# A weight copy moved from GpSimd to a DMA, and a denser output projection for half of a layer

## The chip, the cores and the metric

The kernel runs on one core of one Trainium2 chip. Five engines work side by side, each through its own instructions in order: TensorE (PE in the profile, its weight loads PEld), VectorE (DVE), ScalarE (ACT), GpSimd (POOL) and SyncE (SP), which here issues nearly all DMAs. They wait for one another through semaphores. The metric is the device time in microseconds; lower is better. The time before is 382.32 us, the median of 3 runs (382.29 to 382.58).

## The reference

Two layers of sliding dilated attention alternate with two gated feed-forward layers, all on x of 2048 tokens by 448 channels (bf16), with the same weights both times:

```python
def A(x):   # 16 heads of 28 channels, window of 8 keys, every second token
    q, k, v = split_heads(x @ wqkv)
    idx = pos[:, None] - 2 * arange(8)[None, :]
    attn = softmax(where(idx >= 0, q . k[idx] * 28 ** -0.5, -1e9))
    return merge_heads(attn . v[idx]) @ wo

def B(x):
    return ((x @ w_gate) * (x @ w_up)) @ w_down     # 448 -> 1792 -> 448

x = x + A(layernorm(x)); x = x + B(layernorm(x))
x = x + A(layernorm(x)); x = x + B(layernorm(x))
```

## The kernel before, in words

The four layers are numbered 0 to 3 (0 and 2 attention, 1 and 3 feed-forward). Tokens lie in 16 blocks of 128 (`NBLK`); x stays in `x_sb` through all layers. A layer is worked in chunks of 256 or 512 tokens, and `SEQ` (line 62) interleaves the chunks of different layers, so that TensorE has feed-forward matmuls while an attention chunk waits for softmax.

Everything is recorded as operations with dependencies (`Sched.add`). Which engine does an operation, and in which order each engine goes, is written out by hand-off tables: `ORDER` (line 104) lists operation numbers for each engine, `BANKS` (line 168) the PSUM banks. `Sched.emit` puts out each engine's list with the semaphore waits that the dependencies ask for. An engine never takes a later operation before an earlier one; that holds for SyncE's DMA list too.

TensorE mostly works on the array cut in two halves of 64 rows (line 363): two matmuls run at the same time, and I call such a pair a step. Score matmuls (line 855) and attention-value matmuls (line 889) are short and use small tiles of the array, eight at a time; a group of 64 of them is called a burst. In an entry of `ORDER` such as `551*3.5/349:1+350:1`, steps of other work (here the down projection) are cut into strips of 32 columns (line 366) and put between the parts of a burst; a burst without such strips is called bare here.

The attention of a pair of blocks ends like this. Values times weights (`AV`) go from PSUM to `O_sb` (line 900), a shuffle spreads the denominators (line 918), ScalarE makes their reciprocals by logarithm and exponential (lines 919 and 920), and VectorE multiplies them in and writes `oT` (line 931, called `N`). Then `y_blocks` (line 946 on) does the output projection of two blocks, and `x_block` (line 971) adds it to x on VectorE (line 972).

A head has 28 channels but takes 32 partitions in `oT`, so 16 heads fill 4 chunks of 128 partitions with 4 rows of each 32 unused. In layer 0 the projection runs over these 4 chunks, 512 rows, with zeros in the unused rows of the weights `wo_g`: 8 steps for a pair of blocks. In layer 2 the last four heads are moved into the unused rows: one DMA (line 949, `M0`) stores them from `oT` to DRAM, four (line 953, `M1`) load them back into rows 28 to 31 of each 32, and the weights are put in the same order, in `wo_g` for one block of the pair and in a second copy `wo_h` for the other. That makes 448 rows, 7 steps.

`wo_h` begins as a copy of `wo_g` made by GpSimd (line 556, `c_wh`). Ten small DMAs (`wp`, lines 557 to 569) then fill the unused rows of both. They depend on the copy and on all layer-0 projections (`Y0`), since those need the zeros.

Of the kernel before, what the change touches and what calls it, by code (L numbers as in the profile page):

```python
# [14 lines left out]
NBLK = S // 128  # L15
NCH = S // 512
QB = 120
NQB = 17
# [41 lines left out]
FILL = 9  # L60
ATT_P = 3.0
# [35 lines left out]
def grp_nc(g):  # L97
# [22 lines left out]
    ),  # L120
    "act": (
# [12 lines left out]
    ),  # L134
    "dve": (
# [18 lines left out]
    ),  # L154
    "pool": (
        "18 19 38 20 21 22 23 24 25 26 27 28 29 30 31 32 33 34 35 36 37 92"
# [235 lines left out]
def build(nc, A_x, A_wqkv, A_wo, B_w_gate, B_w_up, B_w_down, out):  # L392
# [25 lines left out]
    wo_g = sb([128, 4, D], bf, "wo_g")  # L418
# [31 lines left out]
    def one(fn, key=None):  # L450
        return [(fn, key)]
# [702 lines left out]
```

## Time and profile before

| | |
|---|---|
| median of 3 runs | 382.32 us |
| the profiled execution's own time | 381.71 us |
| its span, first to last instruction | 380.0 us |
| granted TensorE clock | 1.00 |
| busy: TensorE / VectorE / ScalarE / GpSimd | 374.5 / 283.6 / 206.2 / 6.5 us |

The profile is one execution. A row of groups gives the line of the kernel, engine, operation, what is written and read, and the count, then busy time and the mean duration of one in ns, then the idle time before and what ended it. A timeline row gives start and duration in us. In the chain of waits, each piece is what the next one waited for, or the instruction before it on its engine; "issue" is time in which nothing that the profile shows was waited for.

### The profile page before, as it was taken

To read this page: it belongs to the slowest core of one execution; us is meant where nothing else is said; L and a number is where in the kernel's file an instruction comes from. 1 tells how busy PE (TensorE), PEld (TensorE's weight loads), DVE (VectorE), ACT (ScalarE), POOL (GpSimd) and SP (SyncE) were. 2 spreads that over 40 slices of the span, in tenths; PEclk is the share of its full clock that TensorE was granted. 3 is DMA by queue.
4 is the path that set the end of the run, shared out by engine and by line. 5 is a ranking of instruction groups with operands and counts; after the bars stand their busy time and mean duration, and the time that the engine had idled before them with its cause. 6 is when DMAs were issued, how large, how long until landed. Compare 5 with 4: busy or idle time off the path is not lost.

```text
span 380.0 us, 14476 instructions
## 1 busy us (share of the span) xinstructions
PE 374.5 (99%) x6396; PEld 213.9 (56%) x6396; DVE 283.6 (75%) x640; ACT 206.2 (54%) x393; POOL 6.5 (2%) x26
## 2 busy tenths in 40 slices
PE   8999999999999999999999999999999999999997
PEld 4654487544555444554867765555555444445764
DVE  7999999989795677858677886746998588275423
ACT  5896997655536462535555524547856544134310
POOL 5001000000000000000000000000000000000000
PEclk9999999999999999999999999999999999999999
DMA  7667542500411023151104215310233103302003
GB/s 263 164 152 174 97 120 55 106 10 14 96 29 30 4 54 65 18 83 32 25 15 59 43 28 97 57 27 3 58 68 60 45 3 76 46 2 50 3 2 133
DMA packets 57850, 23.40 MB, mean 62 GB/s; under 512 B 47356, under 2 KB 57788, under 8 KB 57788
## 3 DMA queue, kind: packets, MB, share of 16 engines
q1 hardware_dynamic: 57644, 22.42, 27.5%
q8 instruction: 50, 0.82, 0.9%
q14 instruction: 12, 0.10, 0.1%
q10 hardware_dynamic: 144, 0.06, 0.1%
HBM read 8.91 MB, written 3.24 MB: 32 GB/s over the span
## 4 chain that ended last, share of the span: by engine, by line
PE 92%; ACT 3%; DVE 3%; DMA 1%; issue 0%; SPq 0%; DVEq 0%
PE ps L363 83%; PE ps L366 4%; PE ps L855 2%; PE ps L889 2%; PE ps L1023 1%; ACT E_sb L864 1%; DVE oT L931 1%; DMA x_sb<-in_A_x_dram 1%; ACT qk L730 0%; ACT R_sb L919 0%; ACT R_sb L920 0%; PE ps L635 0%; DVE R_sb L918 0%; DVE E_sb L871 0%; DVE xn_sb L621 0%
## 5 line engine op out<-in xcount | busy, mean ns | idle before, releaser
L363 PE MATMUL ps<-xnTb,WGU 64*128 64x512 bf16 (+1 forms) x1902 | 173.9, 333 | 0.1
L363 PEld LDWEIGHTS ps<-xnTb,WGU 64*128 64x128 bf16 x1902 | 93.4, 94 | 69.1 <-issue 1.0
L1008 ACT ACTIVATE g_sb<-ps 128x512 bf16<-128x512 f32 (+1 forms) x140 | 70.5, 510 | 92.0 <-PE ps L363 85.6
L1011 DVE TENSOR_TENSOR hT<-g_sb,ps 128x512 bf16<-128x512 bf16 (+1 forms) x140 | 78.4, 576 | 49.0 <-ACT g_sb L1008 48.1
L363 PE MATMUL ps<-WD,hT 64*128 64x448 bf16 x786 | 80.4, 350 | 0.0
L363 PEld LDWEIGHTS ps<-WD,hT 64*128 64x128 bf16 x786 | 40.1, 94 | 31.6 <-issue 0.3
L363 PE MATMUL ps<-xnTa,WQK 64*128 64x512 bf16 (+1 forms) x494 | 53.2, 353 | 0.6 <-DVE xnTa L645 0.5
L972 DVE TENSOR_TENSOR x_sb<-x_sb,ps 128x448 bf16<-128x448 bf16 x62 | 36.4, 614 | 19.6 <-PE ps L363 19.5
L864 ACT ACTIVATE E_sb<-ps,shift_sb 128x1024 bf16<-128x1024 f32 (+1 forms) x36 | 37.3, 1069 | 17.1 <-PE ps L855 16.9
L600 DVE BATCH_NORM_STATS2 st<-x_sb 128x6 f32<-128x448 bf16 x64 | 38.2, 616 | 1.2 <-DMA x_sb<-in_A_x_dram 0.7
L621 DVE TENSOR_SCALAR xn_sb<-x_sb,mv,rstd 128x512 bf16<-128x512 bf16 (+1 forms) x64 | 35.0, 569 | 1.5 <-ACT rstd L605 1.2
L363 PEld LDWEIGHTS ps<-xnTa,WQK 64*128 64x128 bf16 x494 | 23.9, 94 | 20.8 <-DVE xnTa L645 0.7
L730 ACT ACTIVATE qk<-ps 128x1024 bf16<-128x1024 f32 (+1 forms) x29 | 27.2, 948 | 13.8 <-PE ps L363 13.5
L363 PE MATMUL ps<-wo_g,oT 64*128 64x448 bf16 x184 | 26.8, 350 | 0.9 <-DVE oT L931 0.9
L871 DVE TENSOR_TENSOR E_sb<-E_sb,MK 128x1024 bf16<-128x1024 bf16 (+1 forms) x36 | 23.1, 657 | 5.2 <-ACT E_sb L864 5.1
L931 DVE TENSOR_TENSOR oT<-O_sb,R_sb 128x480 bf16<-128x480 f32 (+3 forms) x36 | 23.0, 656 | 3.2 <-ACT R_sb L920 3.1
L900 ACT ACTIVATE O_sb<-ps 128x512 f32<-128x512 f32 (+2 forms) x24 | 12.8, 564 | 21.5 <-PE ps L889 21.5
L363 PE MATMUL ps<-WV,xnTa 64*128 64x336 bf16 (+3 forms) x244 | 23.4, 305 | 0.1
L918 DVE STREAM_SHUFFLE R_sb<-O_sb 128x480 f32<-128x480 f32 (+1 forms) x34 | 22.9, 693 | 0.0
L919 ACT ACTIVATE R_sb<-R_sb 128x480 f32<-128x480 f32 (+1 forms) x34 | 19.9, 600 | 4.4 <-DVE R_sb L918 4.2
L920 ACT ACTIVATE R_sb<-R_sb 128x480 f32<-128x480 f32 (+1 forms) x34 | 19.9, 599 | 0.2
L855 PEld LDWEIGHTS ps<-Qz,qk 64*32 64x32 bf16 (+1 forms) x912 | 12.5, 94 | 7.7 <-issue 3.0
(68 smaller groups left out, 232.6 us busy)
## 6 DMA issues: line engine op xcount, KB each, us to landing
out_dram<-x_sb SPq DMA_DIRECT2D x15, 112.0 KB, 1.8
x_sb<-in_A_x_dram SPq DMA_DIRECT2D x3, 448.0 KB, 5.6
hT<-in_A_wqkv_dram SPq DMA_DIRECT2D x4, 224.0 KB, 4.3
WGU<-in_B_w_gate_dram SPq DMA_DIRECT2D x4, 224.0 KB, 3.7
WGU<-in_B_w_up_dram SPq DMA_DIRECT2D x4, 224.0 KB, 3.8
WD<-in_B_w_down_dram SPq DMA_DIRECT2D x2, 448.0 KB, 3.7
WGU<-in_B_w_gate_dram SPq DMA_DIRECT2D x2, 336.0 KB, 4.9
WGU<-in_B_w_up_dram SPq DMA_DIRECT2D x2, 336.0 KB, 4.4
```

The costliest lines, as they stand in the source:

```text
L363: return lambda E: E.matmul(out(), lhs(), rhs(), start=start, stop=stop)
L600: sc.add("dve", one(lambda E, B=B: E.bn_stats(st6[:, B, :], x_sb[:, B, :]), ("bn", li, B)), 525.0, deps=[("x", li - 1, B)] + ([("xn", li - ...
L621: sc.add("dve", one(lambda E, B=B, dst=dst, src=src: E.tensor_scalar(dst, src, mv[:, B, 0:1], rstd[:, B:B + 1], ALU.subtract, ALU.mult), ( ...
L730: return E.activation(dst, src, ACT.Copy) if hasattr(E, "activation") else E.tensor_copy(dst, src)
L855: ins.append((lambda E, hc=hc, c=c, s_=s_, p=p, b=b, h=h, ks=ks, qs=qs, lo=lo, hi=hi: E.matmul(ps[64 * c + KN * s_:64 * c + KN * s_ + KN, ...
L864: return E.activation(E_sb[:, slot, 2 * hp:2 * hp + 2, 0:w], ps[:, b0:b0 + 2, 0:w], ACT.Exp, bias=shift_sb[:, 0:1], scale=SCALE)
L871: return E.tensor_tensor(e, e, MK[:, kind, 0:nc].unsqueeze(1).unsqueeze(1).to_broadcast([128, 2, w // nc, nc]), ALU.min)
L918: sc.add("dve", one(lambda E: E.stream_shuffle(R, Of, [DH] * 32), ("Rs", li, qb)), dve_est(w) + 20.0, deps=[("Oa", li, g)] + prev, prio=prio)
L931: return E.tensor_tensor(oT[:, :, a % HALF:a % HALF + z - a], O[:, :, a - tok:z - tok], R.rearrange("p (h n) -> p h n", h=4)[:, :, a - tok ...
L972: sc.add("dve", one(lambda E: E.tensor_tensor(x_sb[:, B, :], x_sb[:, B, :], ps[:, bk[w], 0:D], ALU.add), ("x", li, B)), dve_est(D), deps=[ ...
L1008: sc.add("act", one(lambda E, gs=gs, bk=bk: E.activation(g_sb[:, gs, 0:nt], ps[:, bk[0], 0:nt], ACT.Copy), ("G", li, j, fc)), act_est(nt), ...
L1011: sc.add("dve", one(lambda E, gs=gs, bk=bk, fc=fc: E.tensor_tensor(hT[:, fc, hs, 0:nt], g_sb[:, gs, 0:nt], ps[:, bk[1], 0:nt], ALU.mult), ...
```

## The change

The copy of `wo_g` into `wo_h` becomes a DMA on SyncE's queue. `Y0`, the projections for which the ten small weight loads wait, shrinks to those of blocks 0 to 7 (`YP = 8`), and blocks 8 to 15 of layer 0 take the branch with 448 rows that layer 2 uses, with its stores and loads of `oT`. The tables `ORDER` and `BANKS` are new throughout. One line is added near the top, so lines behind it count one more in the changed kernel (931 becomes 932).

```diff
+YP = 8
...
-    sem_names += [f"d_p{li}_{j}" for li in (0, 2) for j in range(len(CH[li]))] + [f"d_v{q}" for q in range(NQB)] + ["d_one", "d_stv", "d_wp", "d_wq"]
+    sem_names += [f"d_p{li}_{j}" for li in (0, 2) for j in range(len(CH[li]))] + [f"d_v{q}" for q in range(NQB)] + ["d_one", "d_stv", "d_wp", "d_wq", "d_wh"]
...
-    sc.add("pool", one(lambda E: E.tensor_copy(wo_h[:], wo_g[:, 0:3, :]), "c_wh"), 1900.0, deps=["c_mk2"] + [("wo", j) for j in range(4)], prio=-20)
-    Y0 = [("Y", 0, B) for B in range(NBLK)]
+    plain_dma("sp", wo_h[:], wo_g[:, 0:3, :], "c_wh", "d_wh", deps=[("wo", j) for j in range(4)], prio=-43)
+    Y0 = [("Y", 0, B) for B in range(YP)]
...
-        if li == 0:
+        if li == 0 and B < YP:
             twin_blocks(lambda w: ps[:, bk[w], 0:D], lambda w, c, lo: oT[lo:lo + 64, c, 128 * ((B + w) % 8):128 * ((B + w) % 8) + 128], lambda w, c, lo: wo_g[lo:lo + 64, c, :],
                         (("Y", li, B), ("Y", li, B + 1)), [range(4)], [[]], nd + WOP, prio, bk)
         else:
```

In the new order of SyncE the copy (92) stands just ahead of the last gate load (82), and behind the weights `wo` (84 to 87) that it reads:

```diff
-... 86 84 87 85 71 83 82 89 304 369 302 ...
+... 86 84 87 85 71 83 92 82 89 304 302 367 ...
```

The first weight load for the denser projection (93) stands ahead of the transposes that load v for groups 11 and 12 (527, 526), the store of `oT` for blocks 8 and 9 (546) and its four loads (547 to 550). On TensorE, bursts, their strips and projections have changed places. 35 small copies out of PSUM or of weights change sides between VectorE and ScalarE, 17 to ScalarE and 18 to VectorE.

More of the change, by code (lines that the diff above doesn't have):

```diff
@@ L105 @@
     "pe": (
[14 rows of a table removed]
[14 rows of a table added]
     ),
     "act": (
[12 rows of a table removed]
[12 rows of a table added]
     ),
     "dve": (
[18 rows of a table removed]
[18 rows of a table added]
     ),
     "pool": (
-        "18 19 38 20 21 22 23 24 25 26 27 28 29 30 31 32 33 34 35 36 37 92"
+        "18 19 38 20 21 22 23 24 25 26 27 28 29 30 31 32 33 34 35 36 37"
     ),
     "sp": (
[7 rows of a table removed]
[7 rows of a table added]
     ),
```

132 rows, old and new, of tables (BANKS, ORDER) are left out of this document.

## The prediction

> **What bounds the kernel now.** I read the page first, then the engine sums by stretch, then the chain of waits, and last single rows where the chain leaves TensorE.
>
> ```profile
> span 380.0 us, 14476 instructions
> PE 374.5 (99%) x6396; PEld 213.9 (56%) x6396; DVE 283.6 (75%) x640; ACT 206.2 (54%) x393; POOL 6.5 (2%) x26
> PE 92%; ACT 3%; DVE 3%; DMA 1%; issue 0%; SPq 0%; DVEq 0%
> ```
>
> The chain that ended last lies on TensorE for 92% of 380.0 us. Where it does not, the stretches tell (columns: TensorE, weight loads, VectorE, ScalarE, GpSimd):
>
> ```profile
> 20.00:36.50 16.50, 15.10 (x324) 8.12 (x320) 15.45 (x40) 14.38 (x22) 1.38 (x1) 1.00 0.63 159
> 36.50:50.00 13.50, 13.16 (x338) 7.48 (x340) 12.79 (x29) 11.25 (x17) 0.00 (x0) 1.00 0.50 95
> 50.00:100.00 50.00, 49.95 (x964) 30.77 (x960) 47.07 (x109) 34.68 (x70) 0.00 (x0) 1.00 0.29 64
> 100.00:200.00 100.00, 100.00 (x1664) 54.93 (x1660) 72.89 (x158) 50.11 (x97) 0.00 (x0) 1.00 0.22 38
> ```
>
> From 50 to 200 us TensorE is idle for 0.05 us, and the clock is 1.00. There the time is the amount of TensorE work: only fewer matmuls, or cheaper changes between matmul shapes, can win, and any wait put in its way loses one for one. Between 20 and 50 us it is idle 1.4 + 0.34 us, while VectorE and ScalarE are busy for 85 to 95%: the one stage where other engines set the pace. Its longest wait for another engine in that stage:
>
> ```profile
> PE ps L363 <- DVE oT L931: 0.9, 1, 0.9
> ```
>
> It is the first output projection of layer 0, waiting for the normalised attention output. The chain of waits there, and the rows of VectorE and GpSimd:
>
> ```profile
> 33.09 0.99 ACT R_sb L920 x2
> 34.11 2.34 DVE oT L931 x2
> 36.45 0.05 issue
> 36.49 2.12 PE ps L363 x24
> ...
> 34.11 2.33 DVE L931 TENSOR_TENSOR oT<-O_sb,R_sb 128x480 bf16<-128x480 f32 x2 [0.22 <-ACT R_sb L920]
> ...
> L931 DVE TENSOR_TENSOR oT<-O_sb,R_sb x36: 381/652/1756, 30.3 to 321.0; 128x480 bf16<-128x480 f32 x30, 128x512 bf16<-128x512 f32 x2, 128x224 bf16<-128x224 f32 x2, 128x256 bf16<-128x256 f32 x2
> ...
> 34.55 1.38 POOL L556 COPY wo_h<-wo_g 128x1344 bf16<-128x1344 bf16 x1 [27.87 <-DMA wo_g<-in_A_wo_dram]
> ```
>
> Two multiplies take 2.33 us where the median of one is 652 ns. One of the 36 took 1756 ns; with 2.33 us for the pair it is the second, begun near 34.7. GpSimd's only instruction after its set-up, the copy that the change removes, runs from 34.55 to 35.93. So the copy lies on VectorE's slow multiply, that multiply lies on the chain, and TensorE waits 0.90 us for it.
>
> **The change, part by part.**
>
> *Copy by DMA.* Removed: 1.38 us of GpSimd. If the copy is what held the multiply, that falls back from 1756 to 652 ns, 1.10 us. Both orders put the same TensorE steps ahead of the first projection (its matmuls counted in each: the same number of each shape, and four attention bursts), so TensorE arrives as before and wins at most its wait: **-0.90 us**. Bounds: -0.90, and 0 if the multiply was slow for another reason. I take the full value, as the 1756 ns stands alone among 36 and coincides with the only such copy. The Trainium skill, "SBUF — State Buffer", section "SBUF: two separate sides", has VectorE with two SBUF inputs and a reading GpSimd instruction lock one another out for a whole instruction, and no DMA slowed by an engine or the reverse. By that rule the hold is from about 34.7 to 35.93, some 1.2 us where the row has 1.10; either is more than the 0.90 that TensorE waits, and it is why I give the other reason little.
>
> Added is one DMA on SyncE's queue, just ahead of the last gate load:
>
> ```profile
> 33.75 0.61 SPq L458 DMA_DIRECT2D WGU<-in_B_w_gate_dram  x1
> 37.50 0.40 SPq L458 DMA_DIRECT2D WD<-in_B_w_down_dram  x1
> ...
> WGU<-in_B_w_gate_dram SPq DMA_DIRECT2D x2, 336.0 KB, 4.9
> ...
> 49.74 10.16 PE ps L363 x164
> ```
>
> It waits for wo_g (34.55, where GpSimd's wait ended), and with it the gate load, from 33.75 to about 35.0. That lands 4.9 us later, near 40; the first feed-forward matmul is at 49.74. The load of down weights behind it went only at 37.50, when an earlier load had landed. Cost 0, hidden by nearly 10 us; without that cover 1.25 us. The copy's own landing is needed only by the fifth projection pair, some 45 us later.
>
> *Projection on 448 rows for blocks 8 to 15.* A pair of blocks took 8 steps of two matmuls and now takes 7, as layer 2 already does. Its steps there:
>
> ```profile
> 188.96 0.35 PE L363 MATMUL ps<-wo_g,oT 64*128 64x448 bf16 x1
> 189.34 0.35 PE L363 MATMUL ps<-wo_g,oT 64*128 64x448 bf16 x1
> ```
>
> Two steps lie 0.38 us apart, 0.19 each; four pairs save four steps: **-0.76 us**, all on TensorE's path. It adds per pair one store of oT to DRAM and four loads back, 20 DMAs, and the ten small loads of the re-ordered weights move from 147-182 us to behind the fourth pair. What this may delay is a rival below; its own cost on TensorE I take as 0, by this count. Between the end of the fourth pair and the fifth, the new order has eleven gate/up units of 14 matmuls, a value group, an attention-value burst and a score burst. Prices:
>
> ```profile
> 163.05 1.68 PE L363 MATMUL ps<-xnTb,WGU 64*128 64x512 bf16 x14
> ...
> L750 SPq DMA_TRANSPOSE v_sb<-vt x27: 1093/1232/2683, 54.2 to 299.6; - x27
> L953 SPq DMA_DIRECT2D oT<-mv_rows x32: 242/302/482, 180.1 to 326.4; - x32
> DMA to landing us min/median/max: 1.7/1.9/3.4
> ```
>
> A unit adds about 1.5 us (its last matmul's tail overlaps the next), so 16.5, and with the smaller groups about 18 us. In that time SyncE must issue, in this order, a weight load, two transposes for v, six weight loads, a store of qk rows and its landing, a third transpose, the store of oT and its landing, and four loads and three weight loads and their landing: 16 short issues at 0.35 (5.6), three at 1.27 (3.8), three landings at 1.9 (5.7), together about 15.1 us. Spare: 2.9 us. A rule speaks against this: the Trainium skill, "DMA: Bandwidth & Descriptors", section "Specifications", wants at least 512 B per transfer for line rate, and these move 256 B. Were two landings doubled by that, the count would be 18.9, 0.9 us late, and the gain 0.9 smaller; layer 2's own transfers of this kind are the 1.9 above, so the row decides.
>
> *Orders.* TensorE leaves its 64-row matmuls for the short attention matmuls 35 times before and 33 times after. What a burst costs depends on whether matmuls of other work, cut in 32-column strips, stand in it:
>
> ```profile
> 199.12 0.61 PE ps L889 x64
> 199.74 1.46 PE ps L363 x14
> ...
> 164.73 0.18 PE ps L889 x16
> 164.91 0.19 PE ps L366 x8
> 165.16 0.19 PE ps L366 x7
> 165.38 0.19 PE ps L366 x5
> 165.67 4.47 PE ps L363 x41
> ...
> 48.48 0.57 PE ps L855 x32
> 49.06 0.61 PE ps L889 x64
> ```
>
> A bare burst of 64 runs from 199.12 to 199.74, 0.62 us. One with three strips takes 0.94, of which 0.57 is strip work that would cost the same elsewhere: 0.37. So strips save 0.25 us per burst. Bare value bursts fall from 5 to 3: -0.50. One two-block score burst becomes bare, which the trace does not show for that shape: 0 to +0.25, taken +0.15, as its matmuls stream up to 80 columns where the value burst's stream 64. Of the two visits fewer, one puts a value burst against a score burst of another shape; such neighbours at 48.48 cost 0.57 and 0.61, what they cost alone, so 0. The other joins two value bursts but leaves six groups of eight without a strip: -0.25 to +0.05, taken -0.05. Sum **-0.40**, bounds -0.75 to -0.20.
>
> ScalarE and VectorE exchange copies ahead of the feed-forward. On ScalarE:
>
> ```profile
> L730 ACT ACTIVATE qk<-ps 128x1024 bf16<-128x1024 f32 x24 | 24.3, 1022 | 11.0 <-PE ps L363 10.8
> L730 ACT ACTIVATE qk<-ps 128x512 bf16<-128x512 f32 x5 | 3.0, 592 | 2.8 <-PE ps L363 2.8
> L900 ACT ACTIVATE O_sb<-ps 128x448 f32<-128x448 f32 x10 | 5.4, 538 | 9.9 <-PE ps L889 9.9
> L645 ACT ACTIVATE xnTa<-ps 128x512 bf16<-128x512 bf16 x7 | 4.1, 599 | 0.1
> L525 ACT ACTIVATE WQK<-hT 128x448 bf16<-128x448 bf16 x1 | 0.6, 578 | 0.0
> L795 ACT ACTIVATE v_sb<-ps 128x224 bf16<-128x224 f32 x2 | 0.7, 357 | 0.0
> ```
>
> Of qk, one of 1024 and three of 512 columns come and two of 1024 go (+0.75); two O_sb (+1.0, by their mean) and one v_sb (+0.36) come; one xnTa and one WQK go (-1.18): about +0.9 us. ScalarE is idle (16.5 - 14.38) + (13.5 - 11.25) = 4.4 us between 20 and 50, so I take 0; bounds -0.3 (TensorE's idle 0.34 us behind the first projection goes too) to +0.9.
>
> The sum: -0.90 - 0.76 - 0.40 = -2.06 us, span 377.9. The profiled execution took 381.71 with 380.0 in the span; it would take 379.65. The median of the runs shown, 382.32, lies 0.61 above it, so I forecast 382.32 - 2.06 = **380.3**.
>
> **Rivals.**
>
> 1. ScalarE becomes the bound of the first 50 us. The 0.90 won at the first projection is lost again before 50 us, and its 0.9 us more comes out on TensorE's path: -2.06 + 1.8 = -0.26, 382.1. For it: TensorE is idle 0.34 us behind that projection too, with ScalarE busy for 85%. Against: ScalarE's 4.4 us idle.
> 2. SyncE's queue is late (slower). Place: the first weight load, which now waits for the fourth projection pair while three transposes, the oT store and its loads stand behind it. The fifth pair then stalls TensorE, and the matmuls behind it. With every transpose at 2.68 and every landing at 3.4, the count is 5.6 + 8.0 + 10.2 = 23.8, or 5.8 us late: 386.1. It decides from 2.06 us late, a count of 20. For it: such rows exist; against: they are the extremes, and all would have to meet. Midway, 384.2.
> 3. The change does not free VectorE: the multiply is slow for its own reason. Then -1.16: 381.2. For it: nothing but that 1.38 us and one row are all the evidence.
> 4. More than summed: bounds at their better ends, -0.90 - 0.76 - 0.75 - 0.3 = -2.71, 379.6, or 379.2 with some of the small idle bits gone.
>
> **How the numbers follow.** About 0.2% (0.76 us) is what a measurement of this kernel tells from no change: 381.56 to 383.08 is "same". Chances: forecast 0.63 (379.6 to 381.4 by its bounds), rival 1 0.13, rival 2 0.09, rival 3 0.08, rival 4 0.07. Faster is forecast, 3 and 4 less a little that crosses 381.56: 0.76. Same is rival 1 and that little: 0.15. Slower is rival 2: 0.09. The range 379.2 to 382.0 leaves out rival 2, half of rival 1 and a sliver below, about 0.18.
>
> **What would show it.** The copy: GpSimd has nothing after 6.7 us, no multiply of line 932 (931 before) far above 0.65 us, TensorE's 0.9 us wait for oT gone or under 0.2. The projection: 6394 matmuls, oT stores 12 instead of 8, the idle time of TensorE from 50 to 200 us still under 0.3. The bursts: three bare value bursts of 64 in the chain, about 0.6 us each, and one bare score burst. Wrong if TensorE waits for DMA oT near 84 us (rival 2), if its idle time between 36.5 and 50 us grows by over 1 us with ScalarE as releaser (rival 1), or if a slow multiply stays without the copy (rival 3).

## The result, and the profile after

| | before | after |
|---|---|---|
| median of 20 runs each, side by side | 382.51 us (381.73 to 383.21) | 381.25 us (379.76 to 383.25) |
| ratio, 95% interval | | 0.9969 (0.9957 to 0.9981) |
| own time of the profiled execution | 381.71 us | 380.34 us |
| its span | 380.0 us | 378.6 us |

The change gains 1.26 us by the medians, 0.3%. The prediction said 380.3, range 379.2 to 382.0: the direction was right, and 0.8 us of the 2.06 it had summed did not come. (The median lies 0.95 above the forecast, in part because the kernel before took 0.19 more here than the 382.32 that the forecast went by.) The runs of the changed kernel also spread over 3.5 us, those of the kernel before over 1.5.

The head of the page, and the engines' shares of the chain that ended last:

```profile
span 378.6 us, 14480 instructions
PE 374.3 (99%) x6394; PEld 214.1 (57%) x6394; DVE 284.8 (75%) x641; ACT 204.0 (54%) x392; POOL 5.1 (1%) x25
PE 94%; DVE 1%; ACT 0%; issue 0%
```

TensorE is still the bound, with two matmuls fewer, as counted. The stretches (TensorE, weight loads, VectorE, ScalarE, GpSimd):

```profile
20.00:36.50 16.50, 16.23 (x328) 8.41 (x324) 15.06 (x39) 14.76 (x25) 0.00 (x0) 1.00 0.58 145
36.50:50.00 13.50, 13.30 (x350) 8.17 (x348) 12.70 (x30) 12.43 (x20) 0.00 (x0) 1.00 0.74 147
50.00:100.00 50.00, 49.98 (x956) 30.37 (x954) 46.85 (x109) 34.74 (x72) 0.00 (x0) 1.00 0.32 71
100.00:200.00 100.00, 100.00 (x1680) 54.50 (x1676) 74.76 (x159) 48.98 (x93) 0.00 (x0) 1.00 0.22 38
```

TensorE's idle time falls from 1.40 to 0.27 us in the first stretch and from 0.34 to 0.20 in the second; from 50 to 200 us it is 0.02 (0.05 before). All its waits for another engine that the view of waits shows (total, times, longest):

```profile
PE ps L518 <- DVE hT L489: 1.3, 1, 1.3
PE ps L856 <- DVE Qz L842: 0.3, 1, 0.3
```

The wait for `oT` (0.9 us) and one of 0.5 us for `xnTa` are gone; the 1.3 us at the start was there before. The row of the multiply, and the timeline around it:

```profile
L932 DVE TENSOR_TENSOR oT<-O_sb,R_sb x36: 384/652/693, 30.8 to 319.3; 128x480 bf16<-128x480 f32 x30, 128x512 bf16<-128x512 f32 x2, 128x224 bf16<-128x224 f32 x2, 128x256 bf16<-128x256 f32 x2
```

```profile
34.22 1.23 DVE L932 TENSOR_TENSOR oT<-O_sb,R_sb 128x480 bf16<-128x480 f32 x2 [0.86 <-ACT R_sb L921]
...
35.24 0.55 SPq L459 DMA_DIRECT2D wo_h<-wo_g  x1
...
35.66 0.93 PE L364 MATMUL ps<-wo_g,oT 64*128 64x448 bf16 x8
35.84 0.62 SPq L459 DMA_DIRECT2D WGU<-in_B_w_gate_dram  x1
```

The slowest of 36 multiplies takes 693 ns instead of 1756, and the pair 1.23 us instead of 2.33. The copy's DMA waits for `wo_g` until 35.24, and the gate load behind it goes at 35.84 instead of 33.75; nothing waits for it.

The prediction costed the change on three parts of TensorE's time. I split the time of both profiles in the same way: a step is taken at what it takes undisturbed (109, 189 and 216 ns for 256, 448 and 512 columns); what the steps of a burst and its two neighbours take beyond that is the cost of the bursts; the rest is waits and small gaps. A wait that falls into a burst or beside it counts with the burst.

| us | before | after | difference | predicted |
|---|---|---|---|---|
| undisturbed steps | 359.69 | 358.93 | -0.76 | -0.76 |
| bursts | 11.04 | 10.98 | -0.05 | -0.40 |
| the rest | 5.46 | 4.86 | -0.60 | -0.90 |
| sum | | | -1.41 | -2.06 |

The largest parts of the rest: from 20 to 36 us -0.82 (the wait for `oT`), from 100 to 250 us -0.54, and from 250 to 300 us +0.59, where TensorE is held four times for 0.14 to 0.26 us (at 265.9, 270.1, 277.6 and 297.6). At three of these the last thing that the trace shows is a PSUM bank freed by VectorE or ScalarE just before; at 277.6 it shows none.

Three bursts of the chain, pieces with start and duration (line 890 is the values, 856 the scores, 367 the strips between their parts):

```profile
48.08 0.65 PE ps L890 x64
...
89.27 0.61 PE ps L856 x55
...
205.70 0.15 PE ps L890 x8
205.85 0.19 PE ps L367 x8
206.04 0.03 PE ps L890 x8
206.07 0.11 PE ps L367 x8
206.18 0.12 PE ps L890 x16
206.30 0.12 PE ps L367 x5
206.41 0.03 PE ps L890 x3
206.44 0.11 PE ps L367 x5
206.55 0.29 PE ps L890 x22
206.84 4.23 PE ps L364 x55
```

Bare value bursts are down to three, as said (29.14, 41.77 and 48.08). But the burst at 205.70 has four strips and gains nothing: 1.14 us less 0.53 of strips is 0.61, what a bare one takes.

### The profile page after: what moved, and what is told of

Read it like the earlier page. It is cut to its first block, busy times and chain, and to the rows that moved or that the text cites. A ratio compares the mean times of both kernels' runs of the same rounds, so it can differ in the third digit from the quotient of the medians.

```text
span 378.6 us, 14480 instructions
## 1 busy us (share of the span) xinstructions
PE 374.3 (99%) x6394; PEld 214.1 (57%) x6394; DVE 284.8 (75%) x641; ACT 204.0 (54%) x392; POOL 5.1 (1%) x25
## 4 chain that ended last, share of the span: by engine, by line
PE 94%; DVE 1%; ACT 0%; issue 0%
PE ps L364 84%; PE ps L367 4%; PE ps L856 2%; PE ps L890 2%; PE ps L1024 1%; PE ps L636 0%; DVE xn_sb L622 0%; DVE Qz L842 0%; DVE st L601 0%; DVE mv L603 0%; ACT qk L731 0%; ACT lnv L604 0%; DVE x_sb L1028 0%; DVE xnTa L646 0%; DVE qmask L514 0%
## 5 line engine op out<-in xcount | busy, mean ns | idle before, releaser
L364 PEld LDWEIGHTS ps<-xnTb,WGU 64*128 64x128 bf16 x1892 | 95.4, 94 | 67.3 <-DVE x_sb L973 1.7
L364 PE MATMUL ps<-WD,hT 64*128 64x448 bf16 x800 | 82.3, 349 | 0.0
L364 PEld LDWEIGHTS ps<-WD,hT 64*128 64x128 bf16 x800 | 39.0, 94 | 33.1 <-issue 0.4
L731 ACT ACTIVATE qk<-ps 128x1024 bf16<-128x1024 f32 (+1 forms) x31 | 28.1, 914 | 9.5 <-PE ps L364 9.4
L932 DVE TENSOR_TENSOR oT<-O_sb,R_sb 128x480 bf16<-128x480 f32 (+3 forms) x36 | 22.0, 627 | 2.9 <-ACT R_sb L921 2.6
L842 DVE TENSOR_SCALAR Qz<-qk,qmask 128x960 bf16<-128x960 bf16 (+1 forms) x36 | 14.7, 451 | 5.0 <-ACT qk L731 3.7
L901 ACT ACTIVATE O_sb<-ps 128x448 f32<-128x448 f32 (+2 forms) x22 | 11.7, 549 | 12.3 <-PE ps L890 12.2
```

The costliest lines, as they stand in the source:

```text
L364: return lambda E: E.matmul(out(), lhs(), rhs(), start=start, stop=stop)
L731: return E.activation(dst, src, ACT.Copy) if hasattr(E, "activation") else E.tensor_copy(dst, src)
L932: return E.tensor_tensor(oT[:, :, a % HALF:a % HALF + z - a], O[:, :, a - tok:z - tok], R.rearrange("p (h n) -> p h n", h=4)[:, :, a - tok ...
```

## The experiments

**The copy.** Theory A: GpSimd's copy holds the multiply, and TensorE's wait of 0.9 us goes with it. Theory B: the multiply is slow for its own reason. Three kernels: the kernel before with nothing but the DMA copy; the kernel before with the copy still on GpSimd, but behind the sixth projection pair; and the changed kernel with the copy back on GpSimd.

```diff
copy_dma_only, against before
-    sc.add("pool", one(lambda E: E.tensor_copy(wo_h[:], wo_g[:, 0:3, :]), "c_wh"), 1900.0, ...)
+    plain_dma("sp", wo_h[:], wo_g[:, 0:3, :], "c_wh", "d_wh", deps=[("wo", j) for j in range(4)], prio=-43)
copy_gpsimd_late, against before
-... "c_wh"), 1900.0, deps=["c_mk2"] + [("wo", j) for j in range(4)], prio=-20)
+... "c_wh"), 1900.0, deps=["c_mk2", ("Y", 0, 11)] + [("wo", j) for j in range(4)], prio=-20)
after_copy_gpsimd, against after
-    plain_dma("sp", wo_h[:], ...)
+    sc.add("pool", one(lambda E: E.tensor_copy(wo_h[:], ...
```

> The kernel before with one thing changed: the copy of wo_g into wo_h is a DMA, ahead of the last gate load on SyncE's queue; all orders as before. Theory A (GpSimd's copy held VectorE's multiply on TensorE's path): no multiply of line 931 above 0.75 us, TensorE's 0.9 us wait for oT gone, span 0.7 to 1.0 us shorter, so 0.998 of the time before. Rival B (the new orders, not the copy, removed the wait; the multiply was slow for its own reason): one multiply stays near 1.7 us, the wait stays, no change.

> The kernel before with the copy still on GpSimd, but made to wait for the projection of block 11, so that it runs near 101 us, where VectorE is busy for about 73%. Theory A: the multiply near 34.7 us takes 0.65 us, TensorE's wait goes, and the time falls by 0.7 to 1.0 us as with the DMA, unless a VectorE instruction that is urgent near 101 us is held for up to 1.4 us there; some instruction with two inputs in SBUF then shows a long row near 101 us. Rival B: no change, the multiply stays near 1.7 us.

> The changed kernel with the copy put back on GpSimd, the rest as changed. In the changed kernel's trace the second multiply runs from 34.80 to 35.45 us and the first projection begins at 35.66; the copy would begin near 34.6 and end near 35.9. Theory A: that multiply ends near 36.4, the projection begins 0.7 to 0.9 us later, span 0.6 to 0.9 us longer. Rival B: no change beyond 0.2 us.

| | median | ratio to before | slowest multiply |
|---|---|---|---|
| copy_dma_only | 381.66 us (9 runs) | 0.9978 (0.9968 to 0.9988) | 693 ns |
| copy_gpsimd_late | 381.49 us (11 runs) | 0.9972 (0.9962 to 0.9981) | 692 ns |
| after_copy_gpsimd | 381.05 us (12 runs) | 0.9970 (0.9956 to 0.9984) | 691 ns |

The median before in this comparison is 382.44: -0.78 and -0.95 us for the first two, and neither has TensorE's wait for `oT`. The row of the late copy:

```profile
103.34 1.30 POOL L556 COPY wo_h<-wo_g 128x1344 bf16<-128x1344 bf16 x1 [96.69 <-PE ps L363]
```

The same GpSimd instruction costs nothing where no such multiply is near. So the collision costs, not the engine. The third kernel says the same by a miss: it should have lost 0.6 to 0.9 us. The rows of its copy and its multiplies, from two stretches of its timeline:

```profile
35.95 1.30 POOL L557 COPY wo_h<-wo_g 128x1344 bf16<-128x1344 bf16 x1 [29.38 <-DMA wo_g<-in_A_wo_dram]
...
34.76 1.23 DVE L932 TENSOR_TENSOR oT<-O_sb,R_sb 128x480 bf16<-128x480 f32 x2 [0.86 <-ACT R_sb L921]
```

In this execution SyncE issues the loads of `wo_g` from 32.05 us instead of 30.24; GpSimd starts 1.4 us later than before, when the last of the two multiplies (to 35.99) is all but over. In the changed kernel's own profile the loads go from 30.85 and the DMA that reads `wo_g` at 35.24, also behind the start of the second multiply (34.80); in the kernel before GpSimd began ahead of it, at 34.55 against 34.68. So in the two executions of the new order that show it, the order alone avoids the collision, and the DMA avoids it a second time.

**The 448 rows.** Theory A: four steps of 0.19 us and no more. One kernel undoes them in the changed kernel, one puts half of them into the orders of before (blocks 12 to 15, with the DMA copy).

```diff
after_512_rows, against after: the small weight loads moved behind the last projection of layer 0
-YP = 8
+YP = 16
rows448_old_orders, against before with the DMA copy: stores and loads of oT for two pairs added to SyncE's order
+YP = 12
```

> The changed kernel with the projection of blocks 8 to 15 of layer 0 back on 512 rows (8 steps a pair) and no stores and loads of oT there; the ten small weight loads go behind the last of these projections; the orders otherwise as changed. Theory A (the saved steps are on TensorE's path and their DMAs are hidden): 4 steps of 0.19, so 0.76 us longer. Rival C (the stores and loads, or their place on SyncE's queue, cost what the steps save): no change, or shorter, within 0.3 us.

> The kernel before with the copy of the output weights made by a DMA and with 448 rows for the last four of the eight row blocks of the first layer's second half that the change makes denser, but the orders of before for all the rest: the part of the change that is not a reordering, with half of its 448-row steps. Theory A (the rewritten orders bring nothing net, -0.05 us in the trace): -0.8 to -0.95 from the copy as in the run with the copy alone (381.66), and two steps of 0.19 fewer, -0.38, together about 381.3 us, the same as the changed kernel within 0.2. Theory B (the orders bring the 0.40 us that the prediction gave them, and the denser projection gives part of its 0.76 back in waits): 381.6 us or more.

Both missed. `after_512_rows` took 383.64 us (10 runs, ratio 1.0022, 1.0008 to 1.0036): 2.4 us over the changed kernel, not 0.76. Its undisturbed steps are up by exactly 0.76; the rest is up by 2.7, of which 2.0 are two gaps of a kind taken up below. `rows448_old_orders` took 388.43 us (5 runs, ratio 1.0161, 1.0141 to 1.0182), 6 us over before. Its waits of TensorE:

```profile
PE ps L364 <- issue: 3.9, 1, 3.9
PE ps L367 <- DMA oT<-mv_rows: 1.4, 1, 1.4
```

Both stand ahead of a denser projection. At the second, the multiply ends at 144.84, the store to DRAM goes at 144.88, the loads from 146.54 to 147.81, and TensorE, at the projection since 145.31, goes on at 149.23. The hop through DRAM takes 4.4 us; with 512 rows there is none, and the old order has only 0.5 us of other work between the multiply and the projection. Behind this wait TensorE's granted clock in the trace is 0.50 for 3.4 us, and its steps of 448 columns take 0.37 us instead of 0.19, which costs another 1.7 us. The two waits, the slow stretch and the two steps saved (-0.38) make 6.6 of the 7.0 us between this profiled execution (388.15) and that of `copy_dma_only` (381.15). The reordering is thus part of the price of the 448 rows. In the changed kernel the first such pair (SyncE's and TensorE's timelines):

```profile
81.83 0.58 SPq L950 DMA_DIRECT2D mv_rows<-oT  x1
...
85.34 0.30 SPq L954 DMA_DIRECT2D oT<-mv_rows  x1
...
92.85 0.35 PE L364 MATMUL ps<-wo_g,oT 64*128 64x448 bf16 x1
```

The last load goes at 85.34; with the median landing of 1.9 us it is there at 87.2, 5.6 us early.

**The strips.** Theory A: a burst is bound by the weight loads of its small tiles, and a strip saves only as much as its columns cover. Theory B: the strips' width doesn't matter. Two bursts of the changed kernel got three strips of 448 or 512 columns each; then the value burst alone.

```diff
after_wide_strips, against after (TensorE's order)
-... 896 984*1.2.4.5/897:1+1045:3 1079 ...
+... 896 984*2.4.5/897:3 1045 1079 ...
-... 478 463 612 457 475 ...
+... 478 463 612*2.4.5/457:3 475 ...
wide_value_burst, against after
-... 896 984*1.2.4.5/897:1+1045:3 1079 ...
+... 896 984*2.4.5/897:3 1045 1079 ...
```

> The changed kernel with two edits of TensorE's order alone: the value burst at about 205.6 us gets three strips of 448 columns and none of the 256-column strips it has now, and the score burst that stands bare at about 89.2 us gets three strips of 448 columns; no operation is added or left out. Theory A (a burst is bound by the weight loads of its small tiles, eight loads of 66 ns where 29 ns would stream, and only a strip long enough to cover the next loads hides them): the first burst goes from 498 to about 250 ns beyond its columns and the second from 429 to about 239, together -0.44 us, about 380.8 us where the changed kernel has 381.25. Theory B (the strips' width does not matter; what a burst costs is the entry and the exit, or depends on what stands around it): both bursts stay within 60 ns of what they cost now, 381.2 us. Theory C (the dense small matmuls at 205 us run TensorE's instruction fetch dry in some executions): wider strips there slow the use of instructions little, so the spread of the times (379.8 to 383.3) stays.

> The changed kernel with one edit of TensorE's order: the value burst at about 205.6 us gets three 448-column strips in place of one of 448 and three of 256; the score burst at 89 us stays bare, because with strips it ran into a wait of 0.48 us for a bank. Theory A (strips save only what their width covers): the burst from 498 to about 257 ns as in the run with both bursts widened, no new wait, so 0.24 us under the changed kernel's time in an execution without a gap in TensorE's instructions, 380.0 to 381.0 us for the median. Theory B (the slower time of the run with both bursts, 382.3 us, came from the value burst at 205 us and not from the score burst and the gap at 288 us): 382 us or more here too.

The chain of `wide_value_burst`:

```profile
205.53 0.18 PE ps L890 x16
205.71 0.19 PE ps L367 x8
205.90 0.06 PE ps L890 x16
205.96 0.19 PE ps L367 x7
206.15 0.03 PE ps L890 x5
206.18 0.19 PE ps L367 x5
206.37 0.11 PE ps L890 x23
206.47 1.62 PE ps L364 x21
208.10 0.54 issue
208.63 2.37 PE ps L364 x28
```

0.94 us less 0.57 of strips is 0.37, against 0.61 with the narrow strips: theory A, and the 0.25 us that the prediction took from a burst with such strips. The starts of single groups of eight matmuls, taken from the trace, show why: in this burst they follow one another in 28 to 35 ns; behind a 256-column strip the next take 48 to 67 ns, and from the fifth on in a bare burst 66 to 67 ns. The columns alone would let a group pass in 29; the pace of 66 is, by theory A, that of its eight weight loads, which have time to run ahead under a strip of 448 columns (189 ns) and not under one of 256 (109 ns).

The two-burst kernel took 382.3 us all the same (12 runs, ratio 0.9988, 0.9974 to 1.0002), and its profiled execution holds two reasons. At the score burst:

```profile
89.22 0.26 PE L856 MATMUL ps<-Qz,qk 64*32 64x64 bf16 x16
89.77 0.41 PE L367 MATMUL ps<-xnTb,WGU 64*32 64x512 bf16 x8 [0.29 <-DVE hT L1012]
```

The strip belongs to a unit whose PSUM bank VectorE frees at 89.7, and the burst stands still for 0.48 us: a strip can only cover if its own bank is free. The other reason is a gap of 1.32 us at 287.7. `wide_value_burst` alone took 380.80 us (10 runs, ratio 0.9957, 0.9942 to 0.9973), as theory A had it, though its profiled execution shows a gap too, the 0.54 us at 208.10. The interval overlaps that of the changed kernel, so it is the trace that shows the 0.25 us and not the times.

**The gaps.** They stand under "issue": TensorE waits for nothing visible. To see whether they make the changed kernel's spread, it was profiled four times more.

> The changed kernel once more, for its spread and for a second profile. Theory A (an execution's time depends on whether TensorE's instruction fetch comes late at about 205 to 210 us, where transposes by DMA and the small matmuls of a value burst meet): median 381.2, times again over some 3 us (380 to 383), and a profile of an execution above 381.2 us would show an idle stretch of TensorE of 0.5 us or more that waits for no other engine. Theory B (the spread is that of the chip of the first comparison): times within 1.5 us as for the kernel before, and no such stretch.

> The changed kernel as it is, one profiled execution, to find out why its executions differ by up to 3.5 us. Theory A (TensorE's instructions come late): an execution above 381.3 us shows stretches in which TensorE waits for nothing visible, just after the landing of a 16 KB piece of instructions, and they account for what it has above 380.3 us; an execution near 380.3 us shows none. Theory B (transfers of data land later in slow executions): the excess stands as waits for DMA or for engines that work on late data. Theory C (all matmuls a little slower): the excess is spread over the span and no single wait is longer than in the fast ones.

> The same execution-to-execution question a second time. Theory A: what it has above 380.3 us is the sum of its stretches without instructions, at about 205 to 210 us or 287 to 289 us, within 0.3 us. Theory B: waits for DMA or for engines hold it. Theory C: no single wait does.

> The same question a third time. Theory A: what it has above 380.3 us is the sum of its stretches without instructions, within 0.3 us. Theory B: waits for DMA or for engines hold it. Theory C: no single wait does.

`after_again` gave a median of 380.30 us (6 runs, 379.90 to 382.24). The chain of `after_look_3`, the longest of the profiled ones, at the place where the changed kernel's first profile runs on without a break:

```profile
207.15 1.35 PE ps L364 x13
208.50 1.00 issue
209.50 1.55 PE ps L364 x23
```

The page lists a DMA queue of its own for instructions (packets, MB, share of 16 engines):

```profile
q8 instruction: 50, 0.82, 0.9%
```

50 packets of 16 KB, one every 7.6 us. TensorE's trace has 12,928 records (12,788 matmuls and weight loads, and 140 semaphore instructions and the like), about 50 times 256. Set beside the gaps:

| profiled execution | own time | packet starts, landed | gap | resumes after landing by |
|---|---|---|---|---|
| after | 380.34 | 204.17, 205.10 | none | |
| after_again | 380.26 | 204.05, 204.98 | none | |
| after_look_1 | 381.06 | 206.23, 207.29 | 0.50 at 208.1 | 1.30 |
| after_look_2 | 381.05 | 206.33, 207.33 | 0.5 at 208.2 | 1.31 |
| after_look_3 | 382.39 | 207.08, 208.02 | 1.00 at 208.5 | 1.48 |
| same, later packet | | 287.88, 288.84 | 0.4 at 289.9 | 1.48 |
| wide_value_burst | 380.82 | 206.35, 207.28 | 0.54 at 208.1 | 1.35 |
| after_copy_gpsimd | 381.24 | 206.75, 207.82 | 0.5 at 208.6 | 1.26 |
| after_512_rows | 383.92 | 207.78, 209.11 | 1.44 at 208.9 | 1.27 |
| same, later packet | | 288.63, 289.97 | 0.6 at 290.6 | 1.25 |
| after_wide_strips | 382.21 | 286.12, 287.57 | 1.32 at 287.7 | 1.42 |
| before | 381.71 | 206.19, 207.12 | none | |

Every one of the nine gaps ends 1.25 to 1.48 us after a packet has landed. And all stand ahead of one of two instructions. Counting every record of TensorE in order of time from 0, these are numbers 7,617 and 10,689, also in the kernels whose orders differ: 3,072 apart, exactly 12 times 256. The same count fits every other packet. If a block of instructions begins at each record 193 + 256k, then in all 14 profiled executions, 686 blocks, none begins sooner than 1.21 us after the k-th packet has landed. TensorE has come to the end of the instructions that it holds, and waits for the next piece. The Trainium skill, "Runtime: NRT & Kernel Launch", section "Instruction fetch mechanics", has an engine's instructions refilled in 16 KiB blocks of 256, as here, and calls the cost of crossing a block mostly hidden; here it is not, up to 1.44 us.

By the count, the kernel before has the same packet no earlier (landed 207.12) and still no gap: it comes to this place in its instructions at 211.2, the changed kernel at 207.9. The block ahead of it, 256 records, lasts 6.7 us there and 4.3 in the changed kernel. The new orders bring the value burst of 210.73 forward to 205.70, so the instruction-hungry steps lie closer together: a burst has 64 matmuls and as many weight loads in 0.6 us, and a strip has 16 instructions where the plain step has 4. The kernel before is held at another block, by 0.19 us (record 8,641 at 242.85, 1.31 us behind its landing).

Why the packet starts near 204.1 us in some executions of the changed kernel and 2.1 to 3.0 us later in others is settled in part. SyncE's rows for one transpose, in the executions `after` (packet at 204.17) and `after_look_3` (at 207.08):

```profile
204.10 2.02 SPq L751 DMA_TRANSPOSE v_sb<-vt  x1
...
205.04 1.23 SPq L751 DMA_TRANSPOSE v_sb<-vt  x1
```

In `after`, `after_again`, `after_wide_strips` and `bare_value_burst` the packet starts within 0.1 us of this transpose, whose issue then takes 1.9 to 2.1 us. In the six executions with a gap at 208 to 210 us the same issue takes 1.2 us, and the packet starts 1.9 to 2.4 us behind its start. So the late packet comes behind this transpose and the early one does not; what decides between the two is open.

The executions of `after` add up so: `after_look_1` and `_2` are 0.75 us over the 380.3 of those without a gap, 0.7 of it at the gap; `after_look_3` is 2.1 over, 1.7 at its two gaps and 0.4 in the first 20 us. Theory A, with a miss of 0.1 us in the last.

One kernel more to test it: the burst at 205.70 without strips, as a bare burst costs the same 0.61 us there but 48 instructions less.

```diff
bare_value_burst, against after
-... 896 984*1.2.4.5/897:1+1045:3 1079 ...
+... 896 984 897 1045 1079 ...
```

> The changed kernel with one edit of TensorE's order: the value burst at about 205.6 us runs bare, with none of its four strips; the strips' columns run as plain steps behind it. A strip is 8 matmuls and 8 weight loads where the plain step is 2 and 2, so 48 of TensorE's instructions fall away just ahead of the gap at 208 us. By its weight loads the burst should cost 497 ns as the bare one at 199 us in the kernel before, and it costs 498 with its narrow strips, so the edit alone should be worth nothing. Theory A (TensorE runs out of instructions at 208 us, because the 16 KB piece lands late, at 207.1 to 209.1, and the dense bursts use up what is there): plain steps use 4 instructions in 0.19 us, so 48 fewer put the point where they run out back by up to 2.3 us; no gap at 208 us in the profile, and a median 0.4 to 0.8 us below the changed kernel's 381.2, 380.4 to 380.8, with a smaller spread. Theory B (the gaps come from something else that lands with the piece, or move to another place): a gap of 0.5 us or more stays in the profile, or the median stays at 381.0 to 381.4.

380.21 us (6 runs, 379.91 to 381.15; ratio 0.9948, 0.9935 to 0.9961). Its chain:

```profile
204.99 0.76 PE ps L364 x8
205.75 0.61 PE ps L890 x64
206.36 4.72 PE ps L364 x63
```

The burst costs 0.61 us, and the critical instruction comes at 209.3 instead of 207.9. A packet that lands at 207.3, as in `after_look_1` and `_2`, would be in time for that; one as late as in `after_look_3` (208.02) just about. But in this execution the packet landed early (205.10), so the profile does not show the cure, and the times do not either. Of 29 runs of the changed kernel (median 381.12), 10 are over 381.5 us, here none of 6; but the changed kernel itself gave 380.30 in the 6 runs of `after_again` (ratio 0.9949, 0.9930 to 0.9968). Whether the bare burst helps is open.

## Why the prediction was right, and where it fell short

**Copy by DMA, -0.90:** right. -0.78 and -0.95 in the two kernels that do this alone, and the stretch from 20 to 36 us gives -0.82. The price of the DMA on SyncE, 0, held: the gate load is 2.1 us later, with the first feed-forward matmul at 48.72. What the prediction did not see is that the new order by itself, in the profiles here, moves the copy out of the way.

**448 rows, -0.76:** right in the steps, which are counted. The count of SyncE's queue was 15.1 us against 18 of TensorE's work, 2.9 spare; measured, 5.6 are spare, so rival 2 never came near. But "its own cost on TensorE I take as 0" holds only for the orders that came along: in the old ones, half the steps cost 5.3 us of waits and 1.7 of a lower clock behind them.

**Orders, -0.40:** the step that failed. "So strips save 0.25 us per burst" was priced on a burst with three strips of 448 columns and applied to all strips; the value burst at 205.70, with three strips of 256 and one of 448, saves nothing (0.61 with them, 0.61 bare). In the score burst at 198.4, two strips of 256 and one of 448 save about half: 0.33 with the way in and out, where wide strips leave 0.24 to 0.26 and a bare one takes 0.45 (at 89.2). With the way in and out counted, the two bare bursts of 0.50 us (at 62.8 and 199.1) became one of 0.33 with two strips of 336 columns and one of 0.36 with two of 448: -0.31 instead of -0.50. And the burst at 210.73, which had wide strips before, went from 0.36 to 0.50 with narrow ones, +0.14, where the prediction had nothing. The smaller terms held: joining a value burst with a score burst 0, joining two value bursts -0.06 (-0.05 predicted), the bare score burst +0.19 (+0.15). The other bursts changed by up to 0.2 us each in both directions and together come to nothing, which is luck. The measured sum is -0.05, outside the bounds.

**ScalarE, 0:** right. It is busy 1.56 us longer from 20 to 50 us (27.19 instead of 25.63, with +0.9 predicted) and TensorE idles less; rival 1 falls.

**Left out:** two costs of packing the work closer. The short waits from 250 to 300 us take 0.59 us, about what the smaller gaps from 100 to 250 us give back (-0.54); that these cancel is luck too. And in executions whose instructions land late, TensorE has gaps of 0.4 to 1 us. Three of five profiled executions of `after` have them; of four with the orders of before, two are held at a block's start, by 0.19 and 0.24 us.

Of the 0.8 us missing from the gain, the two profiles show 0.35 in the bursts and 0.30 in the rest. The remaining 0.15 lies outside the two profiled executions. The runs of the changed kernel have their median 0.9 us above an execution without a gap, but the runs of the kernel before have theirs 0.8 above its profile too, and what makes that up is open. So the gaps explain the spread of the changed kernel; how much of the missing gain they make is open.

## What to carry to other kernels

Price a covering strip by its width against the loads that it has to cover, not by the mean of one burst that worked; and check that its bank is free. When a change adds a hop through DRAM, the order that hides the hop is part of the change and cannot be priced apart. On an engine that is busy 99% of the time, count instructions too: where many small ones lie close together, the supply of instructions is one more resource. A gap for which the profile shows no cause can be told by its place: here, at one of the points that lie 256 records apart, and 1.2 to 1.5 us behind the landing of a packet of instructions.

## What was not expected of the hardware

- TensorE stops at the end of a 16 KB piece of its instructions when the next lands late, and goes on 1.25 to 1.48 us after the landing (nine gaps of 0.4 to 1.44 us, all at the same two numbers in the instruction stream; none of 686 blocks begins sooner than 1.21 us after its packet). The start of the same packet moves by up to 3.0 us between executions of one kernel (204.05 to 207.08), with its place before or behind one transpose by DMA.
- Behind a wait of 3.9 us in `rows448_old_orders`, TensorE's granted clock is 0.50 for 3.4 us. In `after_512_rows`, with its gap of 1.44 us, the clock is 1.00 throughout.
- A GpSimd copy of 128x1344 bf16 takes 1.30 us away from the multiplies (at 103.34) and 1.38 beside the multiplies; the multiply takes 1756 ns beside it and 652 to 693 away from it.
